# First units' queries loaded without zeros, and spread over 128 partitions by GpSimd

## The chip, the core and the metric

The kernel runs on one core of a Trainium2 chip. The time is the device time of one execution in microseconds (us). The kernel before takes 600.12 us, the median of three runs that lie between 600.06 and 600.53.

The engines are named as in the profile: PE is TensorE's matmul, PEld its weight load, DVE is VectorE, ACT is ScalarE, POOL is GpSimd, SP is SyncE, which issues the DMAs (its queue is SPq).

## The reference

Two stages follow each other: attention over chunks of a sequence with a small memory, and a feed-forward layer with a sloped ReLU.

```python
# q, k, v: (4, 8, 768, 64); mem_k, mem_v: (4, 8, 8, 64)
for c in range(768 // 32):
    q_c = q[:, :, c * 32:(c + 1) * 32]
    keys   = mem_k with k[c * 32 - 16 : c * 32 + 32 + 8]     # cut at the ends of the sequence
    values = mem_v with v[the same]
    a = softmax(q_c @ keys.T / 8)
    out[:, :, chunk c] = a @ values
x = out as (3072 tokens, 8 heads * 64)
h = x @ w_in                                   # w_in (512, 2048)
g = max(h, 0) + alpha * min(h, 0)
return g @ w_out                               # w_out (2048, 512)
```

## The kernel before

**Tiling.** The tokens are cut into 8 blocks of 384 (`BT`), and the 8 heads into 4 pairs. A *unit* is one block of one pair of heads, so there are 32 units; unit u is pair u % 4 of block u // 4. A unit has 4 times 96 queries (`TQ`), each of 3 chunks of 32. A key window of a chunk has 64 columns (`KW`: 56 of the sequence and 8 of the memory).

**The first eight units** (`NWIN`) are made in another way than the others, by `load_first`, `score_products` and `windows`, and with them this text is concerned. Their inputs lie ready in an array `first` in memory: for each unit, 128 partitions (two heads of 64) by 1824 columns of 4 bytes: 768 columns of queries (`NQ`), 544 of keys, 512 of values. The queries of a chunk take 64 columns: 32 for the one head, which are zero in the partitions of the other, and 32 for the other head. One matmul over 128 partitions then gives both heads' scores for a chunk, one under the other, with no sum between heads. There are 4 buffers (`early`, `NSET`); units 4 to 7 reuse those of units 0 to 3. These buffers lie where the last four weight blocks will go.

A unit goes through these steps. SP loads queries with keys, then values (L485). TensorE runs a few warming matmuls on a tile of ones (`stir`, L293) and 12 score matmuls (L307, each of them 2 in the profile). VectorE hides what lies outside the sequence, takes the maximum (L504) and subtracts it (`less`, L508, into one of two buffers `e`). ScalarE takes the exponential (L512). VectorE sums (L516) and inverts (L519). GpSimd scales the weights into one of two padded tiles `ew` (L529, L533). TensorE transposes them (`turn`, L541), ScalarE copies the result (L546), TensorE multiplies with the values (L554), and `split` writes the result as a high and a low part (L469 on ScalarE, L472 on VectorE), the input of the feed-forward layer.

**The feed-forward layer** takes 16 blocks of 128 hidden columns for each block of tokens. Its weights come as packed 8-byte words, one DMA of 512 KB for each of `w_in` and `w_out` for a block (L594), and ScalarE and VectorE decode them (`decode_part`: L617, L625, L629, L633, L641, L644) before TensorE uses them (L718 up, L748 down). The later 24 units of attention run in between.

**What sets the order.** The kernel adds each step to a list with its engine, an estimated cost, what it reads and writes, and how much work must follow it (`rest`). `Plan.send` plays this list through with those costs and issues the steps in the order that comes out; a DMA is taken to land 2.3 us after its issue. Each engine runs its own instructions in that order, so an instruction that waits holds up all that stand behind it on its engine. SP is such a queue, too. The costs of the first loads are

```python
step(SP, 1.6, partial(load, 0, NQ + NT * NKT), writes=[("qk", u % NSET)], rest=due(u))
step(SP, 0.78, partial(load, NQ + NT * NKT, NQ + NT * NKT + NV), writes=[("fv", u % NSET)], rest=due(u))
```

Of the kernel before, what the change touches and what calls it, by code (L numbers as in the profile page):

```python
# [9 lines left out]
F32 = mybir.dt.float32  # L10
# [8 lines left out]
P = 128  # L19
B, H, S, D = 4, 8, 768, 64  # L20
NM = 8
CH, LEFT, RIGHT = 32, 16, 8
# [3 lines left out]
NJ = TQ // CH  # L26
TK = LEFT + TQ + RIGHT
BT = 384
NHALF = B * S // BT
NT = BT // TQ  # L30
NPAIR = H // 2
# [36 lines left out]
NKT = TK + 2 * NM  # L68
STARTS = (0, LEFT + CH // 2, TK - 2 * CH + 2 * NM)

PE, DVE, ACT, POOL, SP = "PE", "DVE", "ACT", "POOL", "SP"
# [35 lines left out]

NWIN, NSET = 2 * NPAIR, 4

STARTS_WIN = (0, 2 * LEFT, NKT - KW)  # L110
NQ = NT * NJ * 2 * CH
NV = NT * 2 * D
# [64 lines left out]
def body(ctx: ExitStack, tc: tile.TileContext, qvw, kw, first, w_in, w_out, alpha, out):  # L177
    nc = tc.nc
# [12 lines left out]
    tmp = ctx.enter_context(tc.tile_pool(name="tmp", bufs=1))  # L191
# [9 lines left out]
    qk = [const.tile([P, BT + NT * NKT], F32, name=f"qk{i}") for i in range(NKB)]  # L201
# [5 lines left out]
    early = [wps[NF - NSET + i, 0].tile([P, NQ + NT * NKT + NV], F32, name="early", tag="w") for i in range(NSET)]  # L207
# [7 lines left out]
        nc.gpsimd.memset(e[:, :, KW:], 1e-9)  # L215
    for ew in ews:
        nc.gpsimd.memset(ew, 0.0)
    warm = sm.tile([P, 1], F32, name="warm")
    nc.vector.memset(warm, 0.0)
    nc.scalar.activation(out=warm, in_=warm, func=AF.Exp)  # L220
# [2 lines left out]
    step = plan.add  # L223
# [20 lines left out]
    def rest(place):  # L244
        wide = NNARROW * NF
        return (len(ORDER) - max(place, wide)) * WIDE_PAIR + max(wide - place, 0) * PAIR

    def begins(u):

        return u // NPAIR if u < NWIN else BEGIN[(u - NWIN) // 2]  # L250

    def due(u, later=0):

        return rest(begins(u) + later + (5.5 if u >= FIRST_FRONT else 0))
# [35 lines left out]
    def stir(t, num):  # L290

        for _ in range(num):
            nc.tensor.matmul(out=t, lhsT=busy[:, :P], rhs=busy, start=True, stop=True)  # L293

    def score_products(u):
        blk, pr = divmod(u, NPAIR)
        st = state[u]
        s_ps = ps_s.tile([P, 512], F32, name="s_ps", tag=f"s{u % 2}")
        stir(s_ps, STIR[0] if u == 0 else STIR[1])
        st["s"] = s_ps[:, :2 * NJ * KW].rearrange("p (n k) -> p n k", k=KW)  # L300
        t = early[u % NSET]
        q = t[:, :NQ].rearrange("p (c x) -> p c x", c=NT * NJ)
        keys = t[:, NQ:NQ + NT * NKT].rearrange("p (t k) -> p t k", t=NT)
        for n in range(2 * NJ):
            for i in range(2):
                t, j = n // NJ * 2 + i, n % NJ
                nc.tensor.matmul(  # L307
                    out=st["s"][i * 2 * CH:(i + 1) * 2 * CH, n],
                    lhsT=q[:, t * NJ + j],
                    rhs=keys[:, t, STARTS_WIN[j]:STARTS_WIN[j] + KW],  # L310
                    start=True, stop=True,
                )
# [167 lines left out]
    def load_first(u):  # L480
        blk, pr = divmod(u, NPAIR)
        t = early[u % NSET]

        def load(lo, hi):
            nc.sync.dma_start(out=t[:, lo:hi], in_=first[blk, pr, :, lo:hi])  # L485

        state[u] = {}
        step(SP, 1.6, partial(load, 0, NQ + NT * NKT), writes=[("qk", u % NSET)], rest=due(u))
        step(SP, 0.78, partial(load, NQ + NT * NKT, NQ + NT * NKT + NV), writes=[("fv", u % NSET)], rest=due(u))

    def windows(u):

        st = state[u]
        sk, tks, ak = ("s", u % 2), [("o", 0), ("o", 1)], ("o", 2) if u % 2 else "a"
# [53 lines left out]
        def values():  # L548
# [3 lines left out]
            for t in range(NT):  # L552
                for h2 in range(2):
# [4 lines left out]
                        start=True, stop=True,  # L558
                    )

        step(PE, 1.2, partial(score_products, u), reads=[("qk", u % NSET)], writes=[sk], rest=due(u))
        step(DVE, 0.66, top, writes=[sk, ("mx", u % 3)])
        step(DVE, 0.55, less, reads=[sk, ("mx", u % 3)], writes=e_keys(u))
        step(ACT, 0.52, exps, writes=e_keys(u))
# [24 lines left out]
    def load_w(f):  # L589
        def load(i):  # L590
            k, j = ((f, i), 0) if f < NAPART else ((f, 0), i)
            if k not in raw:
                raw[k] = wps[k].tile([P, 2 if f >= NAPART else 1, DM, 2], I32, name="w_t", tag="w")
            nc.sync.dma_start(out=raw[k][:, j].rearrange("p m b -> p (m b)"), in_=srcs[i][f])  # L594

        i = f - NF + NSET
        after = [("qk", i), ("fv", i)] if i >= 0 else []
        for i in range(2):
            step(SP, 1.31, partial(load, i), writes=[("r", f, i)] + after, rest=rest(place_of(f)))

    def place_of(f):
        return PLACE[0, f]
# [229 lines left out]
    def unit_begins(u):  # L832
        if u < NWIN:
            windows(u)
        else:
            if u % 2 == 0:
                scores([u, u + 1])
        if u < NWIN and u + NSET < NWIN:
            load_first(u + NSET)
        elif u >= NWIN - NKB and u + NKB < NU:  # L840
            load_unit(u + NKB)

    for u in range(NSET):
        load_first(u)
        if u == 1:
            step(SP, 0.6, partial(nc.sync.dma_start, out=al, in_=alpha), writes=["al"])
            step(DVE, 0.1, partial(nc.vector.tensor_scalar, out=rise, in0=al, scalar1=-1.0, scalar2=1.0, op0=ALU.mult,
                                    op1=ALU.add), reads=["al"], writes=["rise"])
    for f in range(NF - NSET):
        load_w(f)  # L850
# [3 lines left out]
    for f in range(NF - NSET, NF):  # L854
        load_w(f)
# [10 lines left out]
    for blk, f in ORDER:  # L866
# [25 lines left out]
        o = o_ps.setdefault((blk, f1), [])  # L892
# [12 lines left out]
def _layout(q, k, v, mem_k, mem_v, moe_w_in, moe_w_out, moe_alpha):  # L905
    import numpy as np

    nh = S // BT
    qT = q.reshape(B, NPAIR, 2, nh, BT, D).transpose(0, 3, 1, 2, 5, 4)
    pad = ((0, 0), (0, 0), (LEFT, RIGHT), (0, 0))  # L910
    kp, vp = np.pad(k, pad), np.pad(v, pad)

    def keys(x, mem, s, *spans):
        return np.concatenate([mem if p is None else x[:, :, s + LEFT + p[0]:s + LEFT + p[1]] for p in spans], axis=2)

    kwin = np.stack([keys(kp, mem_k, t * TQ, (-16, 16), None, (16, 72), None, (72, 104)) for t in range(S // TQ)],
                    axis=2)
    kwin = kwin.reshape(B, NPAIR, 2, nh, NT, NKT, D).transpose(0, 3, 1, 2, 6, 4, 5)
    vwin = np.stack([keys(vp, mem_v, t * TQ, (-16, 16), None, (16, 104)) for t in range(S // TQ)], axis=2)
    vwin = vwin.reshape(B, NPAIR, 2, nh, NT, P, D).transpose(0, 3, 1, 5, 4, 2, 6)  # L920
    nwin = NWIN // NPAIR
    qd = np.zeros((nwin, NPAIR, 2, D, NT * NJ, 2, CH), q.dtype)
    for h in range(2):
        qd[:, :, h, :, :, h] = qT.reshape(NHALF, NPAIR, 2, D, NT * NJ, CH)[:nwin, :, h]
    kfirst = np.stack([keys(kp, mem_k, t * TQ, (-16, 16), None, (16, 104), None) for t in range(S // TQ)], axis=2)
    kfirst = kfirst.reshape(B, NPAIR, 2, nh, NT, NKT, D).transpose(0, 3, 1, 2, 6, 4, 5)
    kfirst = kfirst.reshape(NHALF, NPAIR, P, NT * NKT)[:nwin]
    vparts = vwin.reshape(NHALF, NPAIR, P, NV)
    return dict(
        qvw=np.concatenate([qT.reshape(NHALF, NPAIR, P, BT), vparts], axis=3),  # L930
        kw=np.ascontiguousarray(kwin).reshape(NHALF, NPAIR, P, NT, NKT),
        first=np.concatenate([qd.reshape(nwin, NPAIR, P, NQ), kfirst, vparts[:nwin]], axis=3),
        w_in=np.ascontiguousarray(moe_w_in.reshape(NK, P, NF, P).transpose(2, 1, 0, 3)
                                  ).reshape(NF, P, NK * P).view(np.int64),
        w_out=np.ascontiguousarray(moe_w_out.reshape(NF, P, DM)).view(np.int64),
        alpha=np.ascontiguousarray(moe_alpha.reshape(NF, P).T),
    )
# [15 lines left out]
```

## Time and profile before

| | |
|---|---|
| median of three runs | 600.12 us |
| the profiled execution | 600.83 us |
| its span, first to last instruction | 599.0 us |
| PE busy | 592.1 us (99%) |
| DVE busy | 388.2 us (65%) |
| ACT busy | 211.1 us (35%) |
| POOL busy | 36.7 us (6%) |
| DMA read and written | 41.95 and 6.29 MB |

A row of the timeline or of the groups has the start or the busy time, the engine, the line, the operation, the tile written and those read (`out<-in`), and the shapes. In square brackets, or behind the last bar, stands how long the engine stood idle just before, and what ended this idle time. The busy time of TensorE is modelled at its ends, since matmuls are pipelined: a TensorE that is shown as busy may still have small gaps. Views by stage give the busy time of each engine in a stretch. The DMA rows give size and time from issue to landing.

### The profile page before, as it was taken

The page shows a single profiled execution, that of the slowest core. Times are in us where ns is not written, and L with a number is a line of the kernel's source. Part 1 is how long each engine was busy: PE and PEld are TensorE (multiplying, and loading weights), DVE is VectorE, ACT ScalarE, POOL GpSimd, SP SyncE. Part 2 cuts the span into 40 slices and gives each one's busy share as a digit, 9 for nine tenths or more (in the row PEclk, how much of TensorE's full clock was granted, in tenths as well). Part 3 has the DMA queues.
Part 4 walks back from the last instruction along what each step waited for, and adds up shares of the span by engine and source line. Part 5 has one row for each costly group of instructions (what it writes and reads, how often), then busy time and mean ns, then how long its engine had stood idle before and what let it go on. Part 6 is the DMA issues. An engine that isn't in the chain of part 4 may idle for free.

```text
span 599.0 us, 10981 instructions
## 1 busy us (share of the span) xinstructions
PE 592.1 (99%) x4430; PEld 506.3 (85%) x4430; DVE 388.2 (65%) x904; ACT 211.1 (35%) x580; POOL 36.7 (6%) x61
## 2 busy tenths in 40 slices
PE   8999999999999999999999999999999999999997
PEld 5689898988988989899898888888888888888886
DVE  5888998887958768785885852861762771530530
ACT  3688878644222414323233301302400411210201
POOL 3410000010001101010010100100100100000000
PEclk9999999999999999999999999999999999999999
DMA  8999500222040302403204003003201000000001
GB/s 325 354 402 407 236 0 1 66 65 89 2 146 8 100 5 98 143 11 100 84 17 143 11 1 92 9 0 101 69 2 36 0 1 36 36 1 0 1 1 71
DMA packets 21076, 48.96 MB, mean 82 GB/s; under 512 B 2464, under 2 KB 5792, under 8 KB 21024
## 3 DMA queue, kind: packets, MB, share of 16 engines
q1 hardware_dynamic: 20880, 48.12, 22.7%
q8 instruction: 35, 0.57, 0.4%
q10 hardware_dynamic: 144, 0.13, 0.1%
q14 instruction: 17, 0.14, 0.1%
HBM read 41.95 MB, written 6.29 MB: 81 GB/s over the span
## 4 chain that ended last, share of the span: by engine, by line
PE 96%; DMA 2%; DVE 1%; ACT 1%; issue 0%; SPq 0%; ACTq 0%
PE h_ps L718 44%; PE o_ps L748 44%; PE a_ps L433 3%; PE s_ps L332 2%; DMA w_t<-w_in 2%; PE s_ps L293 1%; PE s_ps L307 1%; PE a_ps L554 0%; DVE w_t L629 0%; ACT qk L546 0%; PE o_ps L541 0%; ACT a L617 0%; DVE w_t L625 0%; DVE xl L472 0%; SPq L485 0%
## 5 line engine op out<-in xcount | busy, mean ns | idle before, releaser
L718 PE MATMUL h_ps<-xh,w 128*128 128x384 f32 (+1 forms) x896 | 248.8, 359 | 0.3 <-DVE w L644 0.3
L718 PEld LDWEIGHTS h_ps<-xh,w 128*128 128x128 f32 x896 | 164.8, 188 | 16.6 <-DVE w L644 0.6
L748 PE MATMUL o_ps<-w,gh 128*128 128x512 f32 x528 | 162.7, 389 | 0.0
L718 PE MATMUL h_ps<-xl,w 128*128 128x384 f32 (+1 forms) x448 | 162.6, 363 | 0.1
L727 ACT ACTIVATE g<-h_ps 128x384 f32<-128x384 f32 (+1 forms) x112 | 60.7, 542 | 194.4 <-PE h_ps L718 128.6
L730 DVE SCALAR_TENSOR_TENSOR g<-g,rise,h_ps 128x384 f32<-128x384 f32 (+1 forms) x112 | 74.8, 668 | 74.5 <-ACT g L727 73.6
L748 PEld LDWEIGHTS o_ps<-w,gh 128*128 128x128 f32 x528 | 99.1, 188 | 20.4
L408 DVE STREAM_TRANSPOSE pt<-e 32x64 f32<-32x64 f32 (+1 forms) x336 | 99.4, 301 | 7.4 <-POOL e L387 2.0
L748 PE MATMUL o_ps<-w,gl 128*128 128x512 f32 x264 | 102.8, 389 | 0.0
L718 PEld LDWEIGHTS h_ps<-xl,w 128*128 128x128 f32 x448 | 84.1, 188 | 10.2 <-DVE xl L472 0.3
L748 PE MATMUL o_ps<-w,xh 128*128 128x512 f32 x240 | 74.8, 393 | 0.0
L748 PEld LDWEIGHTS o_ps<-w,gl 128*128 128x128 f32 x264 | 49.6, 188 | 10.2
L472 DVE TENSOR_TENSOR xl<-a_ps,xh 128x384 fp32r<-128x384 f32 x32 | 17.7, 557 | 59.5 <-ACT xh L469 58.8
L748 PEld LDWEIGHTS o_ps<-w,xh 128*128 128x128 f32 x240 | 45.0, 188 | 8.9
L469 ACT CAST xh<-a_ps 128x384 fp32r<-128x384 f32 x32 | 15.0, 481 | 95.7 <-PE a_ps L433 93.7
L736 DVE CAST gh<-g 128x512 fp32r<-128x512 f32 (+1 forms) x72 | 28.8, 401 | 30.6 <-PE o_ps L748 28.2
L387 POOL TENSOR_TENSOR e<-e,den 128x384 f32<-128x384 f32 x24 | 22.7, 947 | 419.8 <-DVE den L384 270.0
L740 DVE TENSOR_TENSOR gl<-g,gh 128x512 fp32r<-128x512 f32 (+1 forms) x72 | 46.6, 648 | 1.7
L366 ACT ACTIVATE e<-s_ps,mx 128x64 f32<-128x64 f32 x144 | 43.4, 318 | 11.1 <-DVE mx L358 11.1
L748 PE MATMUL o_ps<-w,xl 128*128 128x512 f32 x120 | 46.8, 390 | 0.0
L366 ACT ACTIVATION_READ_ACCUMULATOR e<-s_ps,mx 128x1 f32 x144 | 30.4, 211 | 0.0
L805 ACT COPY o_t<-o_ps 128x512 f32<-128x512 f32 x21 | 12.2, 591 | 44.6 <-PE o_ps L748 44.1
(58 smaller groups left out, 382.6 us busy)
## 6 DMA issues: line engine op xcount, KB each, us to landing
w_t<-w_in SPq DMA_DIRECT2D x16, 512.0 KB, 10.1
w_t<-w_out SPq DMA_DIRECT2D x16, 512.0 KB, 10.0
qk<-kw SPq DMA_DIRECT2D x24, 272.0 KB, 4.4
v_t<-qvw SPq DMA_DIRECT2D x24, 256.0 KB, 2.9
out<-o_t SPq DMA_DIRECT2D x23, 256.0 KB, 2.1
early<-first SPq DMA_DIRECT2D x8, 656.0 KB, 6.3
qk<-qvw SPq DMA_DIRECT2D x24, 192.0 KB, 4.9
early<-first SPq DMA_DIRECT2D x8, 256.0 KB, 6.9
```

Source lines behind the costliest of these rows:

```text
L366: nc.scalar.activation(out=st["e"][:, i], in_=st["s"][h2][:, n], func=AF.Exp, scale=SCALE, bias=d["mx"][:, u - us[0], n, h2:h2 + 1], accum ...
L387: nc.gpsimd.tensor_tensor(out=st["e"], in0=st["e"], in1=st["den"].broadcast_to([P, NJ * 2, KW]), op=ALU.mult)
L408: nc.vector.transpose(out=pts[u % NPT][quad * CH:(quad + 1) * CH, j, t0:t0 + n1 - n0].rearrange("p t h q -> p (t h) q"), in_=(st["e"], zer ...
L433: nc.tensor.matmul(out=st["a"][h2 * D:(h2 + 1) * D, t * TQ:(t + 1) * TQ], lhsT=st["v"][:, t, h2, :], rhs=pts[u % NPT][:, :, t, h2, :], sta ...
L469: nc.scalar.copy(out=ring[k][0][:, cols], in_=st["a"][:, :BT])
L472: nc.vector.tensor_tensor(out=ring[k][1][:, cols], in0=st["a"][:, :BT], in1=ring[k][0][:, cols].bitcast(F32), op=ALU.subtract)
L718: nc.tensor.matmul(out=h["ps"][:, :n_cols], lhsT=ws[f, 0][:, wk, k * P:(k + 1) * P], rhs=parts(blk, k)[1](xk), start=(k == 0 and n == 0), ...
L727: nc.scalar.activation(out=h["g"], in_=h["ps"][:, :n_cols], func=AF.Relu, scale=-1.0)
L730: nc.vector.scalar_tensor_tensor(out=h["g"], in0=h["g"], scalar=rise[:, f:f + 1], in1=h["ps"][:, :n_cols], op0=ALU.mult, op1=ALU.add)
L736: copy(out=h["gh"], in_=h["g"])
L740: nc.vector.tensor_tensor(out=h["gl"], in0=h["g"], in1=h["gh"].bitcast(F32), op=ALU.subtract)
L748: nc.tensor.matmul(out=o_ps[tt], lhsT=h[gk][:, tt * P:(tt + 1) * P], rhs=ws[f, 1][:, wk], start=(f == first_f and i == 0), stop=(f == last ...
```

## The change

The array `first` holds the queries without zeros: 384 columns of 128 partitions instead of 768. They are loaded into a tile of their own (`q_t`, in buffers that are otherwise used late for outputs). Zeros are written once into the halves of the four `early` buffers that have to be zero, by eight memsets on VectorE at the program's start (64 partitions by 384 columns each). For each unit GpSimd then copies each head's 64 partitions by 384 columns from `q_t` to its half of `early`. The keys become a DMA of their own. So a unit is loaded by three DMAs (192, 272 and 256 KB) instead of two (656 and 256 KB).

The columns of the queries are ordered anew: head, query of the chunk, chunk, where it was chunk, head, query. The 64 columns of one score matmul's stationary operand are now 12 columns apart. The score products wait for the copies as well as the keys, and the planner gets new steps with new costs. No arithmetic changes.

```diff
@@ body
     for ew in ews:
         nc.gpsimd.memset(ew, 0.0)
+    for t in early:
+        for h2 in range(2):
+            nc.vector.memset(t[(1 - h2) * D:(2 - h2) * D, h2 * BT:(h2 + 1) * BT], 0.0)
     warm = sm.tile([P, 1], F32, name="warm")
@@ score_products
-        q = t[:, :NQ].rearrange("p (c x) -> p c x", c=NT * NJ)
+        q = t[:, :NQ].rearrange("p (x c) -> p c x", c=NT * NJ)
@@ load_first
+        d = {}
+
         def load(lo, hi):
-            nc.sync.dma_start(out=t[:, lo:hi], in_=first[blk, pr, :, lo:hi])
+            nc.sync.dma_start(out=t[:, lo:hi], in_=first[blk, pr, :, lo - BT:hi - BT])
+
+        def load_q():
+            d["q"] = tmp.tile([P, BT], F32, name="q_t", tag=f"o{u % NSET}")
+            nc.sync.dma_start(out=d["q"], in_=first[blk, pr, :, :BT])
+
+        def spread(h2):
+            rows = slice(h2 * D, (h2 + 1) * D)
+            nc.gpsimd.tensor_copy(out=t[rows, h2 * BT:(h2 + 1) * BT], in_=d["q"][rows])
 
         state[u] = {}
-        step(SP, 1.6, partial(load, 0, NQ + NT * NKT), writes=[("qk", u % NSET)], rest=due(u))
-        step(SP, 0.78, partial(load, NQ + NT * NKT, NQ + NT * NKT + NV), writes=[("fv", u % NSET)], rest=due(u))
+
+        step(SP, 0.53, load_q, writes=[("tmp", u % NSET)], rest=due(u))
+        for h2 in range(2):
+            step(POOL, 0.45, partial(spread, h2), reads=[("tmp", u % NSET)], writes=[("fq", h2, u % NSET)], rest=due(u))
+        step(SP, 0.75, partial(load, NQ, NQ + NT * NKT), writes=[("qk", u % NSET)], rest=due(u))
+        step(SP, 0.7, partial(load, NQ + NT * NKT, NQ + NT * NKT + NV), writes=[("fv", u % NSET)], rest=due(u))
@@ windows
-        step(PE, 1.2, partial(score_products, u), reads=[("qk", u % NSET)], writes=[sk], rest=due(u))
+        step(PE, 1.2, partial(score_products, u), reads=[("qk", u % NSET)] + [("fq", h2, u % NSET) for h2 in range(2)], writes=[sk], rest=due(u))
@@ load_w
-        after = [("qk", i), ("fv", i)] if i >= 0 else []
+        after = [("qk", i), ("fv", i), ("fq", 0, i), ("fq", 1, i)] if i >= 0 else []
@@ _layout
-    qd = np.zeros((nwin, NPAIR, 2, D, NT * NJ, 2, CH), q.dtype)
-    for h in range(2):
-        qd[:, :, h, :, :, h] = qT.reshape(NHALF, NPAIR, 2, D, NT * NJ, CH)[:nwin, :, h]
+    qfirst = qT.reshape(NHALF, NPAIR, P, NT * NJ, CH)[:nwin].swapaxes(3, 4).reshape(nwin, NPAIR, P, BT)
```

Since the planner gets other steps, it sends instructions in another order in the first part of the program. Three places follow. The first is SP's queue up to the first weights: `early_157` to `early_160` are the buffers of units 0 to 3 and then 4 to 7, and 1312 columns are queries with keys. Before:

```order
5 L485 DMA early_157<-first 128x1312
6 L485 DMA early_158<-first 128x1312
7 L485 DMA early_157<-first 128x512
8 L485 DMA early_159<-first 128x1312
9 L485 DMA early_158<-first 128x512
10 L594 DMA w_t_327<-w_in 128x1024
```

And now, where 384 columns are queries, 544 keys and 512 values:

```order
9 L495 DMA q_t_247<-first 128x384
10 L491 DMA early_157<-first 128x544
11 L491 DMA early_157<-first 128x512
12 L495 DMA q_t_276<-first 128x384
13 L491 DMA early_158<-first 128x544
14 L491 DMA early_158<-first 128x512
15 L495 DMA q_t_307<-first 128x384
16 L491 DMA early_159<-first 128x544
17 L612 DMA w_t_326<-w_in 128x1024
```

Ahead of these stand the first loads of units 0 to 3, four DMAs before and eight now. In both orders the queries and keys of seven units and the values of two come before the first weights, in smaller pieces now.

The second place is GpSimd's queue after its first memsets, where `ew0` and `ew1` are the padded tiles of units 0 and 1. Before:

```order
11 L217 MEMSET ew0_161 128x768
12 L217 MEMSET ew1_162 128x768
13 L529 TENSOR_TENSOR ew0_161<-e_167,den_248 128x2x2x64
14 L533 TENSOR_TENSOR ew0_161<-e_167,den_248 128x2x56
15 L533 TENSOR_TENSOR ew0_161<-e_167,den_248 128x2x8
16 L529 TENSOR_TENSOR ew1_162<-e_168,den_273 128x2x2x64
```

And now, with a pair of copies for each unit (`x2`):

```order
16 L499 COPY early_160<-q_t_224 64x384 x2
17 L499 COPY early_157<-q_t_247 64x384 x2
18 L547 TENSOR_TENSOR ew0_161<-e_167,den_274 128x2x2x64
19 L551 TENSOR_TENSOR ew0_161<-e_167,den_274 128x2x56
20 L551 TENSOR_TENSOR ew0_161<-e_167,den_274 128x2x8
21 L499 COPY early_158<-q_t_276 64x384 x2
22 L547 TENSOR_TENSOR ew1_162<-e_168,den_305 128x2x2x64
23 L551 TENSOR_TENSOR ew1_162<-e_168,den_305 128x2x56
24 L551 TENSOR_TENSOR ew1_162<-e_168,den_305 128x2x8
25 L499 COPY early_159<-q_t_307 64x384 x2
```

The copies of units 0 to 4 stand ahead of the first scaling, those of unit 5 ahead of the second, and those of unit 6 ahead of the third.

The third place is VectorE's queue between the inverse for unit 1 and the maximum of unit 4; `e_167` and `e_168` are the two buffers of the exponentials (even and odd units). Before:

```order
16 L519 RECIPROCAL den_273<-den_273 128x6
17 L508 TENSOR_TENSOR e_167<-s_ps_233,mx_270 128x6x64
18 L516 TENSOR_REDUCE den_315<-e_167 128x6
19 L508 TENSOR_TENSOR e_168<-s_ps_254,mx_279 128x6x64
20 L519 RECIPROCAL den_315<-den_315 128x6
21 L502 MEMSET s_ps_295 64x8
22 L504 TENSOR_REDUCE mx_332<-s_ps_295 128x6
23 L516 TENSOR_REDUCE den_345<-e_168 128x6
24 L508 TENSOR_TENSOR e_167<-s_ps_295,mx_332 128x6x64
```

And now:

```order
20 L537 RECIPROCAL den_305<-den_305 128x6
21 L526 TENSOR_TENSOR e_167<-s_ps_258,mx_300 128x6x64
22 L526 TENSOR_TENSOR e_168<-s_ps_284,mx_312 128x6x64
23 L534 TENSOR_REDUCE den_366<-e_167 128x6
24 L520 MEMSET s_ps_332 64x8
25 L522 TENSOR_REDUCE mx_371<-s_ps_332 128x6
26 L537 RECIPROCAL den_366<-den_366 128x6
27 L534 TENSOR_REDUCE den_386<-e_168 128x6
28 L537 RECIPROCAL den_386<-den_386 128x6
29 L476 TENSOR_TENSOR xl_185<-a_ps_373,xh_184 128x384
30 L526 TENSOR_TENSOR e_167<-s_ps_332,mx_371 128x6x64
```

The subtraction for unit 3 moved ahead of the sum of unit 2, the inverse for unit 2 behind the maximum of unit 4, and the subtraction for unit 4 behind the inverse for unit 3 and unit 0's low part.

More of the change, by code (lines that the diff above doesn't have):

```diff
@@ L931, in _layout @@
         kw=np.ascontiguousarray(kwin).reshape(NHALF, NPAIR, P, NT, NKT),
-        first=np.concatenate([qd.reshape(nwin, NPAIR, P, NQ), kfirst, vparts[:nwin]], axis=3),
+        first=np.concatenate([qfirst, kfirst, vparts[:nwin]], axis=3),
         w_in=np.ascontiguousarray(moe_w_in.reshape(NK, P, NF, P).transpose(2, 1, 0, 3)
```

## The prediction

> **What bounds the kernel now.** I first asked for the busy time of each engine by stage, to see where time can be lost at all. The columns are the stretch, its length, and the busy time of PE, PEld, DVE, ACT and POOL, then the granted clock, the DMA share and GB/s.
>
> ```profile
> 0.00:36.00 36.00, 32.83 (x414) 22.87 (x416) 25.89 (x62) 20.09 (x41) 14.01 (x37) 1.00 0.93 347
> 36.00:100.00 64.00, 64.00 (x329) 58.10 (x326) 56.44 (x79) 53.42 (x69) 0.00 (x0) 1.00 0.52 208
> 100.00:200.00 100.00, 100.00 (x935) 89.72 (x934) 79.53 (x194) 41.06 (x133) 5.98 (x6) 1.00 0.20 66
> 500.00:590.00 90.00, 90.00 (x423) 74.44 (x422) 30.99 (x50) 13.38 (x24) 0.00 (x0) 1.00 0.04 16
> ```
>
> From 36 us on TensorE has no gap, and the change alters nothing that TensorE does there. So the time moves by as much as the moment at which TensorE becomes gapless, near 35 us. That TensorE is 99% busy over the whole says little; only the first 36 us count. The same view in steps of 5 us:
>
> ```profile
> 5.00:10.00 5.00, 4.72 (x79) 3.15 (x78) 3.27 (x10) 1.04 (x2) 0.27 (x1) 1.00 1.01 409
> 10.00:15.00 5.00, 4.64 (x73) 3.49 (x74) 3.90 (x12) 2.48 (x7) 2.85 (x8) 1.00 0.97 349
> 15.00:20.00 5.00, 4.79 (x83) 3.33 (x81) 3.10 (x9) 1.82 (x5) 2.49 (x8) 1.00 1.03 400
> 20.00:25.00 5.00, 4.55 (x70) 3.40 (x64) 4.42 (x10) 3.56 (x10) 1.34 (x3) 1.00 0.88 289
> 25.00:30.00 5.00, 4.69 (x52) 3.78 (x52) 4.78 (x12) 4.58 (x11) 2.60 (x5) 1.00 1.00 371
> 30.00:35.00 5.00, 4.88 (x52) 3.91 (x51) 4.93 (x9) 4.48 (x9) 2.33 (x5) 1.00 0.99 382
> ```
>
> DMA runs at its ceiling of about 409 GB/s nearly throughout. VectorE is full from 25 to 35 us (9.71 of 10), but has 1.9 us free between 15 and 20 and 0.58 between 20 and 25. Third, the chain of waits in order of time (start, length, what):
>
> ```profile
> 10.15 9.20 DMA w_t<-w_in
> 19.35 0.02 issue
> 19.37 0.02 ACT a L617
> ...
> 34.20 0.48 DVE xl L472
> 34.68 0.04 issue
> 34.72 0.79 PE h_ps L718 x3
> ```
>
> The chain runs through the first weight load, which takes 9.20 us to land behind the queries, keys and values, and ends at VectorE handing TensorE its last late tile. The timeline tells who stands still for these loads:
>
> ```profile
> 15.58 0.48 ACT L469 CAST xh<-a_ps 128x384 fp32r<-128x384 f32 x1 [0.29 <-PE a_ps L554]
> 17.89 0.56 DVE L508 TENSOR_TENSOR e<-s_ps,mx 128x384 f32<-128x384 f32 x1
> 18.11 0.88 PE L554 MATMUL a_ps<-qk,early 128*64 128x96 f32 x16 [0.21 <-DMA early<-first]
> 19.37 0.69 ACT L617 ACTIVATE a<-w_t 128x512 f32<-128x512 f32 x1 [2.89 <-DMA w_t<-w_in]
> 20.10 0.75 DVE L625 COPY w_t<-w_t 128x512 int16<-128x512 int16 x1 [1.66 <-ACT a L617]
> 21.28 0.56 DVE L516 TENSOR_REDUCE den<-e 128x6 f32<-128x390 f32 x1 [0.43 <-ACT e L512]
> 21.85 0.88 PE L554 MATMUL a_ps<-qk,early 128*64 128x96 f32 x16 [0.33 <-DVE den L516]
> ```
>
> ScalarE's wait of 2.89 us for the weights makes VectorE stand for 1.66 us, and the exponential that ScalarE does late costs VectorE 0.43 us more. TensorE loses only 0.21 and 0.33 us at the value products: its order has other work there.
>
> **What is removed: bytes.** A unit's first load shrinks from 656 KB (768 query and 544 key columns of 4 bytes on 128 partitions) to 192 + 272 KB. Over 8 units that is 1536 KB, 3.85 us at 409 GB/s. By SP's order, the loads up to and including the first weights were 7 x 656 + 2 x 256 + 512 = 5616 KB and become 7 x 464 + 2 x 256 + 512 = 4272 KB: 1344 KB or 3.4 us less, so the weights land near 16.0 instead of 19.35. In ScalarE's new order their first use follows the L469 cast that ended at 15.58 + 0.48 = 16.06, so the 2.89 us wait goes. Unit 1's values land some 4.5 us sooner by the same sum (5104 against 3296 KB ahead), so TensorE's 0.21 us goes too. The loads behind are helped, but 36 us and later has no wait to save.
>
> **What is added at the start.** Rows that price it: issue to landing of the first load (alone in its 0.9 us window) and of the least crowded 256 KB transfers, then the first instructions.
>
> ```profile
> early<-first SPq DMA_DIRECT2D x1, 656.0 KB, 4.0
> ...
> v_t<-qvw SPq DMA_DIRECT2D x24, 256.0 KB, 2.9
> out<-o_t SPq DMA_DIRECT2D x23, 256.0 KB, 2.1
> ...
> 0.74 9.36 SPq L485 DMA_DIRECT2D early<-first  x9
> 0.91 0.48 DVE L200 MEMSET busy<- 128x512 bf16 x1 [0.91 <-PEq L944]
> 1.32 1.41 POOL L217 MEMSET ew<- 128x768 f32 x2
> 1.45 3.60 PE L293 MATMUL s_ps<-busy 128*128 128x512 bf16 x8 [1.45 <-DVE warm L219]
> 4.98 1.41 PE L307 MATMUL s_ps<-early 128*64 128x64 f32 x24
> 6.58 0.56 DVE L504 TENSOR_REDUCE mx<-s_ps 128x6 f32<-128x384 f32 x1
> ```
>
> Eight memsets of 64x384 on VectorE: by columns 0.48 x 384/512 = 0.36 us at least, 0.48 at most; I take 0.4, together 3.2 us, from 1.39 to 4.6 (5.2 at most). VectorE's next work was at 6.47, so this costs nothing; without that cover it would cost 3.2 us. The first query load lands at 0.74 + 2.1 to 2.9, about 3.4 us; GpSimd is free from 1.32 + 1.41 = 2.73. Two copies follow. A copy's price is not in the trace; it lies between writing alone and two inputs:
>
> ```profile
> 30.50 0.42 POOL L578 MEMSET e<- 128x384 f32 x1
> ...
> L387 POOL TENSOR_TENSOR e<-e,den 128x384 f32<-128x384 f32 x24 | 22.7, 947 | 419.8 <-DVE den L384 270.0
> ```
>
> I take 0.5 of 0.42 to 0.95, since one input is read and nothing computed. The copies end near 4.4 (3.7 to 5.5). Keys, 464 KB in, land before the old load's 4.74. TensorE's warming matmuls last to 1.45 + 3.60 = 5.05 anyway: the first score stays at 5.0, cost 0 (at most +0.5).
>
> **What is added later.** Sixteen copies are 8 us on GpSimd (6.7 to 15.2), which worked 1.17 us a unit. Those of units 4 to 7 stand in GpSimd's queue ahead of the softmax scaling of units 0, 1, 2 and 4; behind them wait the transposes on TensorE. SP issues 8 more DMAs (9 took 9.36 us with their waits), and the query loads of units 4 to 7 wait for the copies of units 0 to 3, with keys, values and weights behind. The last of these queries lies 1584 KB in, 928 KB or 2.3 us behind the old first load's landing at 0.74 + 4.0 = 4.74, so the copies end near 7.1 + 1.0 = 8.1, and what is queued stays bound by bytes.
>
> The planner also moves VectorE's `less` (L508 before, L526 now) of unit 3 ahead of the sum of unit 2. It must wait for GpSimd's scaling of unit 1, which reads the same buffer:
>
> ```profile
> 9.73 0.62 POOL L529 TENSOR_TENSOR ew<-e,den 128x256 f32<-128x256 f32 x1 [7.00 <-DVE s_ps L500]
> ...
> 12.55 0.54 POOL L533 TENSOR_TENSOR ew<-e,den 128x112 f32<-128x112 f32 x2
> ...
> 29.02 1.23 DVE L625 COPY w_t<-w_t 128x512 int16<-128x512 int16 x1 [0.17 <-ACT a L617]
> ```
>
> With the durations above: `less` 3 at 13.15 to 13.7, sum 2 to 14.25, maximum 4 to 14.9, sum and inverse 3 to 15.8, unit 0's difference (L472 before, L476 now) after 16.06 to 16.65. Unit 2's scaling starts near 15.1 and takes 1.16, so `less` 4 runs 16.65 to 17.2, maximum 5 to 17.85, sum 4 to 18.4, `less` 5 to 18.95. Before, that ended at 17.89 + 0.56 = 18.45: a cost of 0.5. Then comes the weights' copy, at once. It stands beside a GpSimd scaling now; such a copy took 1.23 instead of 0.75 us (0.48).
>
> **Sum.** VectorE's stalls removed, 1.66 + 0.43 = 2.09; order, -0.5; the crowded copy, -0.48: **-1.1 us**. Everything behind it, up to the gapless stretch, is VectorE's full list, so the gain should survive. Its ends: at least TensorE's own waits 0.21 + 0.33 = 0.5, at most 2.1.
>
> The profiled execution took 600.83 with a span of 599.0 (1.83 outside); the three runs have a median of 600.12, so its span would be about 598.3. I subtract from the median: **599.0 us**, its own range 598.0 to 599.6.
>
> **Rivals.** The new query layout puts the 64 columns of one weight load 12 elements, 48 bytes, apart; before they were contiguous. *Slower weight loads* (rival 1, the other side):
>
> ```profile
> L307 PEld LDWEIGHTS s_ps<-early x192: 132/138/232, 5.0 to 23.8; 128*64 128x64 f32 x192
> L748 PEld LDWEIGHTS o_ps<-w,gh 128*128 128x128 f32 x528 | 99.1, 188 | 20.4
> 12.83 0.78 PEld L307 LDWEIGHTS s_ps<-early 128*64 128x64 f32 x24 [0.42 <-issue]
> ```
>
> 64 more columns cost 188 - 138 = 50 ns, 0.8 ns a column. 24 loads in 0.78 us are 32.5 ns apart, less than the 50, so two overlap. If a strided column costs double, a unit needs 24 x 50 / 2 = 0.6 us more, eight units 4.8. TensorE's gaps from 5 to 35 us could take 0.28 + 0.36 + 0.21 + 0.45 + 0.31 + 0.12 = 1.7 of it, up to 2.8 if the modelled ends hide 0.1 at each of some ten waits: +2.0 to +3.1, about 602.7. It decides from 1.35 times a column's price on, where 8 x 0.21 us exceeds the 1.7. Against it: 0.8 ns a column is slow, and nothing here tells whether packing matters at that pace. No read of TensorE in this trace is strided so, hence both ends stay, 0 and +4.8; I lean to 0.
>
> The Trainium skill (SBUF — State Buffer, Door 1: The DMA port swizzle) states 16-byte lines, of which each access that crosses to a new one pays, so that fp32 may step 4 elements for free. By that rule these loads, one line per column, pay, and the time would be rival 1's; the page names no size, and no run here shows it yet.
>
> *GpSimd late, or the loads hidden anyway* (rival 2). At 0.95 us a copy, the first score waits to 0.74 + 2.9 + 1.9 = 5.5 (+0.5), and unit 5's copies, between the scalings of units 0 and 1, end at 9.73 + 1.16 + 1.9 = 12.8, where the scaling of unit 1 ended at 13.09 and needs 1.16 more: 0.9 late. Then -1.1 + 0.5 + 0.9 = +0.3, 600.4. For it: GpSimd stands on the path of every unit; against: 3.06 us a unit still fits the 3.4 between scores.
>
> **How the numbers follow.** Forecast 0.52; rival 1 0.26 (0.03 of it far beyond, up to four times the column's price); rival 2 0.17; more gain than 2.1 (ScalarE's decoding, moved earlier, frees it too) 0.05. A measurement can tell about 0.2%, 1.2 us: below 598.9 is faster, above 601.3 slower. The forecast lies on that edge: 0.24 faster, 0.28 same. With 0.05 from the last case and 0.16 and 0.03 of the rivals within 0.2%, that is 0.29, 0.47 and 0.24. The range 598.0 to 602.9 leaves out about 0.05 below and 0.13 above.
>
> **What would show it.** Right: w_in lands before 17 us; ScalarE's first decode and VectorE's first weight copy without a DMA wait before them; the first score still at 5.0; 24 score loads in 0.78 us; the chain's last VectorE step near 33 us. Wrong: score loads spread over 1.2 us or more (rival 1); GpSimd copies of 0.8 us or scalings that wait for copies (rival 2); weights still landing after 18 us.

## The result, and the profile after

The changed kernel takes **606.89 us** (median of 4 runs, 606.86 to 606.97) against 600.27 for the kernel before on the same chip. The ratio is **1.0109, with an interval of 1.0097 to 1.0121**: it is 6.6 us slower. The forecast was 599.0, and the range ended at 602.9. The profiled execution took 606.92 with a span of 605.1. Two executions of the experiments below were far slower than all others, one of heads_w4 with 2073 us and one of the kernel before with 653 us at a lower clock, and ratios and ranges leave them out.

First the stage views of the changed kernel, columns as before:

```profile
0.00:36.00 36.00, 34.19 (x353) 25.86 (x354) 24.02 (x64) 17.12 (x34) 20.49 (x52) 1.00 0.84 278
50.00:60.00 10.00, 9.42 (x47) 7.89 (x45) 8.75 (x14) 8.80 (x13) 0.00 (x0) 1.00 1.03 408
```

TensorE now has only 1.81 us of gaps in the first 36 us (3.17 before), and a new gap of 0.58 us between 50 and 60 us, where the kernel before had none. A TensorE that is busier and yet ends later does some work more slowly. The weight loads of the score line say which (durations in ns, shortest, median and longest, then the starts):

```profile
L311 PEld LDWEIGHTS s_ps<-early x192: 207/237/240, 5.0 to 29.4; 128*64 128x64 f32 x192
```

One weight load takes 237 ns instead of 138, and the last starts at 29.4 instead of 23.8. The timeline, for one unit's 24 loads and for the steps that the prediction spoke of:

```profile
4.98 1.71 PEld L311 LDWEIGHTS s_ps<-early 128*64 128x64 f32 x24 [0.84 <-POOL early L499]
9.62 1.70 PEld L311 LDWEIGHTS s_ps<-early 128*64 128x64 f32 x24 [0.42 <-issue]
...
1.54 3.90 DVE L221 MEMSET early<- 64x384 f32 x8
3.23 1.06 POOL L499 COPY early<-q_t 64x384 f32<-64x384 f32 x2 [0.50 <-DMA q_t<-first]
11.43 0.62 POOL L547 TENSOR_TENSOR ew<-e,den 128x256 f32<-128x256 f32 x1
19.68 0.73 ACT L635 ACTIVATE a<-w_t 128x512 f32<-128x512 f32 x1
```

The 24 loads of a unit take 1.71 us where they took 0.78: 0.93 more. Only the first unit had taken longer before, 1.27:

```profile
4.98 1.27 PEld L307 LDWEIGHTS s_ps<-early 128*64 128x64 f32 x24 [0.84 <-DMA early<-first]
```

So eight units cost 7 x 0.93 + 0.44 = 7.0 us more. ScalarE's first decode (L635) no longer waits for a DMA, but it is not earlier than before (19.68 against 19.37), since everything behind the scores is late. The weights themselves land at 18.3 instead of the forecast 16.0: their load is issued at 11.87 (10.15 before), behind loads that wait for the late scores to free their buffers. The chain of waits has lost its DMA; a piece of it past the first stage (start, length, what) is new:

```profile
57.11 0.51 ACT xh L754
57.62 0.96 ACT w L659
58.58 0.39 ACT g L745
58.97 0.02 issue
58.99 0.61 DVE g L748
59.60 0.48 DVE xl L758
```

There ScalarE casts decoded weights (L659) ahead of the ReLU part `g` (L745) that VectorE and TensorE need. So two things had to be told apart from what the prediction counted: the weight loads, and the order that the planner makes of the new steps.

### The profile page after: what moved, and what is told of

It is laid out like the page before. It is cut to its first block, busy times and chain, and to the rows that moved or that the text cites. A ratio compares the mean times of both kernels' runs of the same rounds, so it can differ in the third digit from the quotient of the medians.

```text
span 605.1 us, 11029 instructions
## 1 busy us (share of the span) xinstructions
PE 598.9 (99%) x4430; PEld 512.8 (85%) x4430; DVE 391.0 (65%) x912; ACT 211.3 (35%) x580; POOL 43.6 (7%) x77
## 4 chain that ended last, share of the span: by engine, by line
PE 98%; DVE 0%; ACT 0%; issue 0%; ACTq 0%
PE h_ps L736 44%; PE o_ps L766 43%; PE a_ps L437 3%; PE s_ps L311 2%; PE s_ps L336 2%; PE s_ps L297 1%; PE a_ps L572 1%; PE o_ps L559 1%; PE o_ps L297 0%; ACT w L659 0%; DVE g L748 0%; ACT o_t L823 0%; DVE mx L522 0%; ACT xh L754 0%; DVE busy L201 0%
## 5 line engine op out<-in xcount | busy, mean ns | idle before, releaser
L745 ACT ACTIVATE g<-h_ps 128x384 f32<-128x384 f32 (+1 forms) x112 | 60.5, 540 | 194.3 <-PE h_ps L736 128.9
L748 DVE SCALAR_TENSOR_TENSOR g<-g,rise,h_ps 128x384 f32<-128x384 f32 (+1 forms) x112 | 74.9, 669 | 74.0 <-ACT g L745 73.2
```

The lines of the kernel that those rows point to most:

```text
L745: nc.scalar.activation(out=h["g"], in_=h["ps"][:, :n_cols], func=AF.Relu, scale=-1.0)
L748: nc.vector.scalar_tensor_tensor(out=h["g"], in0=h["g"], scalar=rise[:, f:f + 1], in1=h["ps"][:, :n_cols], op0=ALU.mult, op1=ALU.add)
```

## The experiments

All of these kernels do the whole computation. The kernel before, run beside them, has medians of 600.24 to 600.40.

### Only the column order undone (packed)

The change stays, but the 64 columns of a chunk lie side by side again; memsets and copies write 12 runs of 32 columns instead. The order on the engines is that of the change. Here and below, `...` stands for lines left out.

```diff
-        q = t[:, :NQ].rearrange("p (x c) -> p c x", c=NT * NJ)
+        q = t[:, :NQ].rearrange("p (c x) -> p c x", c=NT * NJ)
-            nc.gpsimd.tensor_copy(out=t[rows, h2 * BT:(h2 + 1) * BT], in_=d["q"][rows])
+            nc.gpsimd.tensor_copy(out=t[rows, :NQ].rearrange("p (c h x) -> p c h x", h=2, x=CH)[:, :, h2],
+                                  in_=d["q"][rows].rearrange("p (c x) -> p c x", x=CH))
...
```

> The changed kernel with one thing undone: the 64 columns of a score matmul's weights lie side by side again, so the memsets and GpSimd's copies write 12 runs of 32 columns. Loads, zeros, copies and the order of all engines are those of the changed kernel. Theory 1 (the whole loss is TensorE's weight loads at a step of 48 bytes): 24 score loads take 0.78 us again instead of 1.71, and the time falls from 606.9 to the forecast's 599.0, between 598.0 and 599.6. Rival (the loss comes from the planner's new order, GpSimd's copies or the smaller DMAs): the loads take 0.78 us but the time stays above 604.

Measured: **601.13 us** (11 runs), ratio 1.0014 [1.0006, 1.0023]. Of this kernel:

```profile
L311 PEld LDWEIGHTS s_ps<-early x192: 132/138/227, 5.0 to 23.5; 128*64 128x64 f32 x192
...
11.00 0.62 POOL L548 TENSOR_TENSOR ew<-e,den 128x256 f32<-128x256 f32 x1
17.29 0.69 ACT L636 ACTIVATE a<-w_t 128x512 f32<-128x512 f32 x1 [0.68 <-DMA w_t<-w_in]
37.45 0.39 PE L767 MATMUL o_ps<-w,xl 128*128 128x512 f32 x1
...
50.00:60.00 10.00, 9.26 (x45) 7.51 (x44) 9.03 (x13) 8.15 (x12) 0.00 (x0) 1.00 1.03 408
```

And of the kernel before:

```profile
38.44 0.39 PE L748 MATMUL o_ps<-w,xl 128*128 128x512 f32 x1
...
50.00:60.00 10.00, 10.00 (x54) 9.26 (x53) 9.03 (x13) 8.22 (x12) 0.00 (x0) 1.00 1.03 407
```

The weight loads are back at 138 ns, and 606.89 - 601.13 = 5.8 us with them. The time lies between the two expectations: the strided columns explain most of the loss, but the forecast gain is not there either. It was there for a while: the first weights land at 17.27 instead of 19.35, and the first down product that TensorE does (L767) starts at 37.45, while L748 started at 38.44 in the kernel before. Then TensorE gets through only 45 matmuls between 50 and 60 us, 54 before: the same ScalarE order as in the changed kernel, seen in its chain:

```profile
51.23 0.51 ACT xh L755
51.74 0.96 ACT w L660
52.70 0.40 ACT g L746
53.10 0.02 issue
53.12 0.61 DVE g L749
53.74 0.48 DVE xl L759
```

### Only the column order changed (step2, step3, step4, step6, step12)

The kernel before, with its zeros and its loads, and the 64 columns of a chunk 2, 3, 4, 6 or 12 elements (8 to 48 bytes) apart.

```diff
+STEP = 12
-        q = t[:, :NQ].rearrange("p (c x) -> p c x", c=NT * NJ)
+        q = t[:, :NQ].rearrange("p (g x s) -> p g s x", x=2 * CH, s=STEP)
-                    lhsT=q[:, t * NJ + j],
+                    lhsT=q[:, (t * NJ + j) // STEP, (t * NJ + j) % STEP],
...
```

> The kernel before with the column order alone changed: queries are loaded with their zeros, but the 64 columns of a score matmul's weights lie 12 elements (48 bytes) apart. Theory 1: 24 score loads take 1.7 us, eight units cost 8 x 0.93 = 7.4 us, less what TensorE's gaps take up (1.7 to 2.8): 604.8 to 606.2. Rival: the strided loads are hidden where no copies and no new order come with them: 600.3 within 1.2.

> The kernel before with the columns 4 elements (16 bytes) apart, so each on a 16-byte line of its own, next to those of three other chunks. If the step in bytes decides and 4 fp32 are free, as the Trainium skill (SBUF — State Buffer, Door 1: The DMA port swizzle) says: 24 loads in 0.78 us and 600.3. If one column per line is what pays: 24 loads in 1.7 us and the time of the kernel with a step of 12.

> The kernel before with the columns 2 elements (8 bytes) apart, two columns to a 16-byte line. If a load pays by the line: 24 loads in 0.78 us and 600.3 us. If it pays by bytes spanned: a fraction more, about 0.85 us, and 600.5 to 601. If anything but side by side pays in full: 1.7 us and the time of the kernel with a step of 12.

> The kernel before with the 64 columns of a chunk's weights 3 elements (12 bytes) apart, all else as before. Steps of 8, 16 and 48 bytes gave 138, 217 and 237 ns for one weight load. Theory A (the price is paid once the columns are farther apart than 8 bytes, whatever the distance): 210 ns or more, about 604 us. Theory B (the price rises with the distance between 8 and 16 bytes): 165 to 195 ns, 601 to 602.5 us.

> The kernel before with the 64 columns of a chunk's weights 6 elements (24 bytes) apart, all else as before. Theory A (price flat beyond 16 bytes, with a small rise): 217 to 237 ns for one weight load, 604 to 605.7 us. Theory B (the number of lines touched counts, so that 24 bytes lies between 16 and 48 in proportion): near 222 ns. Theory C (multiples of 16 bytes are the bad case): under 200 ns and under 603 us.

| columns apart | runs | median, us | ratio to before |
|---|---|---|---|
| 4 bytes (before) | | 600.3 | |
| 8 bytes (step2) | 10 | 600.30 | 1.0001 [0.9992, 1.0010] |
| 12 bytes (step3) | 8 | 601.83 | 1.0022 [1.0012, 1.0032] |
| 16 bytes (step4) | 4 | 604.20 | 1.0065 [1.0050, 1.0081] |
| 24 bytes (step6) | 2 | 603.60 | 1.0054 [1.0036, 1.0072] |
| 48 bytes (step12) | 4 | 605.65 | 1.0091 [1.0077, 1.0105] |

The same row of each kernel, from step2, step3, step4, step6 and step12 in this order:

```profile
L308 PEld LDWEIGHTS s_ps<-early x192: 135/138/225, 5.0 to 23.2; 128*64 128x64 f32 x192
```

```profile
L308 PEld LDWEIGHTS s_ps<-early x192: 164/177/223, 5.0 to 25.6; 128*64 128x64 f32 x192
```

```profile
L308 PEld LDWEIGHTS s_ps<-early x192: 193/217/218, 5.0 to 28.4; 128*64 128x64 f32 x192
```

```profile
L308 PEld LDWEIGHTS s_ps<-early x192: 187/208/217, 4.9 to 27.3; 128*64 128x64 f32 x192
```

```profile
L308 PEld LDWEIGHTS s_ps<-early x192: 207/237/243, 5.0 to 29.5; 128*64 128x64 f32 x192
```

The column order alone costs 5.3 us at the change's 48 bytes. The price of a load starts between 8 and 12 bytes and rises with the distance, but not evenly: 24 bytes is a little cheaper than 16 (208 against 217 ns; in the times alone their intervals overlap). What sets it beyond 16 bytes, these five points don't tell. step12, step2 and theory B of step3 came out as expected; step4 lies between its two cases, and step6's 208 ns is outside all three of its theories.

### The packed kernel in before's order (packed_order)

As packed, but the planner is told of one load of queries and keys at the old cost, and of the copies as steps of cost 0 with no delay behind them. TensorE, ScalarE and VectorE then run before's steps in before's order (VectorE with the eight memsets added), and GpSimd does the copies of units 4 to 7 ahead of the scalings of units 1, 2, 3 and 5.

```diff
-        step(SP, 0.53, load_q, writes=[("tmp", u % NSET)], rest=due(u))
+        step(SP, 1.6, load_both, writes=[("qk", u % NSET)], rest=due(u))
-            step(POOL, 0.45, partial(spread, h2), reads=[("tmp", u % NSET)], ...)
+            step(POOL, 0.0, partial(spread, h2), reads=[("qk", u % NSET)], ...)
-        step(SP, 0.75, partial(load, NQ, NQ + NT * NKT), ...)
...
```

> The changed kernel with the columns of a chunk side by side (so the weight loads should stay near 0.78 us per 24) and with the copies told to the planner as steps of cost 0, so that TensorE, ScalarE and VectorE run the steps of before in before's order; on GpSimd the copies stand ahead of the first scalings as before. Theory A (the forecast's gain of some 1 us is there at 37 us, and the planner's other order on ScalarE, the weights' cast ahead of the ReLU part at 51 to 54 us, gives it back): no TensorE gap over 0.2 us between 50 and 60 us, and 599.0 to 599.7 us. Theory B (the gain is lost in the first 36 us, to copies ahead of the scalings on GpSimd and to the queries landing later): TensorE busy under 33.2 of the first 36 us and 600.3 us or more, with or without a gap at 50 us.

Measured: **600.00 us** (11 runs), ratio 0.9993 [0.9984, 1.0002]. Half of each theory holds. Theory A's gap is gone:

```profile
0.00:36.00 36.00, 32.26 (x416) 23.24 (x421) 27.96 (x71) 20.62 (x43) 21.78 (x53) 1.00 0.87 303
5.00:10.00 5.00, 4.01 (x81) 2.57 (x78) 3.81 (x13) 1.25 (x3) 3.32 (x7) 1.00 1.02 352
50.00:60.00 10.00, 10.00 (x52) 9.17 (x52) 9.22 (x13) 8.00 (x11) 0.00 (x0) 1.00 1.03 408
```

52 matmuls instead of 45, at 10.00 / 52 = 0.19 us each, are 1.3 us, and the time fell by 1.13 against packed. So the order was worth that. But 600.00 is 0.3 us under before where theory A has 0.6 to 1.3, and TensorE is busy for only 32.26 of the first 36 us, as theory B has it. Its own reasons, copies ahead of the scalings and late queries, do not show: the first scaling starts at 9.59, before at 9.73, and no unit's scores start later than before. The timeline of this kernel and the chain in order of time show another:

```profile
16.67 0.69 ACT L639 ACTIVATE a<-w_t 128x512 f32<-128x512 f32 x1 [0.34 <-DMA w_t<-w_in]
18.20 0.92 DVE L647 COPY w_t<-w_t 128x512 int16<-128x512 int16 x1
28.71 0.67 ACT L639 ACTIVATE a<-w_t 128x512 f32<-128x512 f32 x1 [1.56 <-DMA w_t<-w_in]
29.41 0.77 DVE L647 COPY w_t<-w_t 128x512 int16<-128x512 int16 x1 [2.29 <-ACT a L639]
```

```profile
20.91 0.83 PE a_ps L576 x16
21.75 0.02 issue
21.76 0.33 SPq L491
22.09 0.04 issue
22.13 6.50 DMA w_t<-w_in
```

The first weights come nearly when they should (decoded from 16.67 instead of 19.37), and VectorE's first weight copy stands at 18.20 instead of 20.10: 1.9 us ahead of the profiled execution of before. But the third weight load is issued at 22.13, behind a value load (L491) that stands in SP's queue until TensorE has done a unit's value products and its buffer is free. The view of SP's waits adds these up (total, times, longest, in us):

```profile
SPq L491 <- PE a_ps L576: 6.6, 4, 2.7
```

VectorE gets there early and waits 2.29 us. At its next steps it is 1.0 us ahead, no more.

How much of this lead is the change's? The profiled execution of before took 600.83, 0.7 us above the median. step2 has the same loads and the same order, its weight loads take 138 ns, and its profiled execution took 600.09, near the median. It is a second look at the start before:

```profile
18.53 0.67 ACT L618 ACTIVATE a<-w_t 128x512 f32<-128x512 f32 x1 [1.92 <-DMA w_t<-w_in]
19.23 0.76 DVE L626 COPY w_t<-w_t 128x512 int16<-128x512 int16 x1 [0.67 <-ACT a L618]
20.40 0.56 DVE L517 TENSOR_REDUCE den<-e 128x6 f32<-128x390 f32 x1 [0.40 <-ACT e L513]
28.76 0.91 DVE L626 COPY w_t<-w_t 128x512 int16<-128x512 int16 x1 [0.79 <-ACT a L618]
37.59 0.39 PE L749 MATMUL o_ps<-w,xl 128*128 128x512 f32 x1
```

Against it packed_order is 1.0 us ahead at the first weight copy and 0.14 at TensorE's first down product (37.45 against 37.59). In step2, too, VectorE already waits 0.79 us for the third weight load.

### Those weight loads issued earlier (packed_order_w4, before_w4)

The second and third weight load are issued ahead of unit 4's value load, which is the first that waits for TensorE's value products. Nothing else moves. The control does the same to the kernel before.

```diff
+        early = [self.weights[0, 1], self.weights[1, 0]]
+        order = [n for n in order if n not in early]
+        i = order.index(self.values[4])
+        for n in order[:i] + early + order[i:]:
+            self.steps[n][2]()
...
```

> The kernel with packed columns in before's order (packed_order, 600.0 us), with one thing moved: on the load queue, the second and third weight load (w_out of slice 0 and w_in of slice 1) are issued ahead of the value load of unit 4, which waits for TensorE to free its buffer. In packed_order the first weights land at 16.65 us instead of 19.35, but these two are issued at 20.4 and 22.1 us, and VectorE then waits 2.29 us for the third. Theory A (the bytes saved become time only if the loads behind them are issued earlier too; an in-order queue that waits for TensorE's buffers holds them): the 2.29 us wait is gone or under 0.5 us, and 598.3 to 599.3 us. Theory B (the wait moves elsewhere, TensorE or VectorE being full by then): 599.7 to 600.3 us. Theory C (the value loads now come late): over 600.3 us.

> The control: the kernel before with its full 656 KB unit loads and only the two weight loads moved ahead of the value load of unit 4. Its transfers run at 409 GB/s without a gap to 20 us, so the queue's order can bring no bytes sooner. Theory A (bytes bound the start there, and the third weight load only comes to be waited for once they are saved): 600.0 to 600.8 us, no difference; 0.5 to 2 us slower if the value loads come late. Theory B (the queue's order alone is worth the gain, with or without the smaller loads): 598.5 to 599.5 us.

Measured: **599.43 us** for packed_order_w4 (11 runs, 599.03 to 599.80), ratio 0.9985 [0.9976, 0.9995]; 600.03 for before_w4, ratio 0.9996 [0.9987, 1.0005]. Of packed_order_w4:

```profile
17.70 0.68 ACT L648 ACTIVATE a<-w_t 128x512 f32<-128x512 f32 x1 [0.96 <-DMA w_t<-w_in]
27.40 0.69 ACT L648 ACTIVATE a<-w_t 128x512 f32<-128x512 f32 x1
28.12 0.76 DVE L656 COPY w_t<-w_t 128x512 int16<-128x512 int16 x1 [0.60 <-ACT a L648]
37.08 0.39 PE L779 MATMUL o_ps<-w,xl 128*128 128x512 f32 x1
```

The wait of 2.29 us shrank to 0.60, and TensorE's first down product starts at 37.08 instead of 37.45, although the first weights are decoded at 17.70 instead of 16.67. This version beats both kernels: 0.9 us under before, about what had been forecast for the change, though just short of the 0.2% that the prediction asked for. Theory A's time is 0.1 off its upper end and the wait 0.1 over its 0.5, but its mechanism is there. With the full loads the same move brings nothing that can be told from no change. The two were run side by side, and their runs don't overlap (599.03 to 599.80 against 599.89 to 600.84): with the weight loads moved, the smaller loads are worth 0.6 us. What the move alone brings is less sure: packed_order ran on another chip, and the intervals of the two ratios overlap.

### No zeros and no copies (heads, heads_w4)

The queries are loaded once, without zeros, with the keys in one load of 464 KB; each score product is done as two, one for each head's 64 partitions.

```diff
+                for h2 in range(2):
+                    rows, at_ = slice(h2 * D, (h2 + 1) * D), (2 * i + h2) * CH
                     nc.tensor.matmul(
-                        out=st["s"][i * 2 * CH:(i + 1) * 2 * CH, n],
-                        lhsT=q[:, t * NJ + j],
+                        out=st["s"][at_:at_ + CH, n],
+                        lhsT=q[rows, t * NJ + j],
...
```

> The kernel before with no zeros at all: queries and keys of a unit in one load of 464 KB instead of 928, no copies and no memsets, and the 12 score products of a unit done as 24, each over the 64 partitions of one head, with 32 weight columns instead of 64; all other work in before's order. Theory A (a score product over 64 partitions costs about what the later head products of the same kind show, some 0.6 us per unit for 24 of them, against 0.78 for the 12 full ones, and the bytes saved let the first weights land near 16 us): 598.0 to 599.2 us. Theory B (24 products cost twice 12, 1.6 us per unit, as the strided columns did): +0.8 us a unit, some of it in TensorE's gaps, 603 to 606 us. Theory C (loads are hidden anyway, nothing else changes): 600.0 to 600.6.

> The kernel without zeros whose score products go head by head (heads, 599.79 us; 48 products of 64 partitions per unit instead of 24 of 128), with the same two weight loads moved ahead of the value load of unit 4. In heads VectorE waits 1.68 us for the third weight load, at 28.2 us. Theory A (the held load is what eats the gain): that wait is gone or under 0.5 us, and 598.2 to 599.2 us. Theory B (another wait takes its place): 599.5 to 600.1 us. Theory C (value loads late): over 600.3 us.

Measured: 599.79 us for heads, ratio 0.9992 [0.9984, 1.0001], and 600.07 for heads_w4 (10 runs), ratio 0.9992 [0.9983, 1.0001]: neither can be told from the kernel before. Theory A's price for the products of heads holds, its time does not. A unit's products, and a row of the value products of unit 1, in the timeline of heads_w4; last, the same row in heads:

```profile
20.53 0.87 PE L315 MATMUL s_ps<-early 64*32 64x64 f32 x48
19.51 0.55 PE L563 MATMUL a_ps<-qk,early 128*64 128x96 f32 x8 [0.74 <-issue]
...
19.22 0.55 PE L555 MATMUL a_ps<-qk,early 128*64 128x96 f32 x8 [0.45 <-issue]
```

48 of them take 0.87 us, where 24 full ones take 0.92 in packed_order. In heads VectorE waits 1.68 us at the same weight load as in packed_order. With the loads moved (heads_w4) that wait is 0.67, but TensorE stops for 0.74 us in the middle of a unit's value products, where it stopped for 0.45 before the move. The time is theory B's; its mechanism, another wait in place of the one removed, is seen only in part. What TensorE stops for is open: the row names only "issue", and the values of this unit had landed by 16.5 (issued at 10.59, 5.9 us), so they did not come late.

### The strided kernel in before's order (after_order)

The edit of packed_order, made to the changed kernel, whose columns stay 48 bytes apart.

> The changed kernel, its weight columns 48 bytes apart as in the change, with only the order of the steps put back to before's (the copies told to the planner as steps of cost 0, as in packed_order). Theory A (the two costs add up: 1.1 us for the planner's order, as between packed at 601.13 and packed_order at 600.00, and the rest for the strided weight loads): the ScalarE stall at 57 us is gone and 605.5 to 606.0 us, about step12's 605.65. Theory B (with the strided loads TensorE is full from 5 us on, and the order matters only where it is not): 606.6 to 607.1 us.

Measured: **605.80 us** (4 runs, 605.75 to 606.03), ratio 1.0093 [1.0076, 1.0110]. Theory A: TensorE has no gap from 36 to 100 us, and the order is worth 606.89 - 605.80 = 1.1 us here as well. step12, with before's loads and zeros, took 605.65: with strided columns the bytes saved bring nothing.

## Why the prediction was wrong

The four kernels with and without strided columns, in the new and the old order, make the balance, in medians:

| | strided columns | columns side by side | difference |
|---|---|---|---|
| the planner's new order | 606.89 | 601.13 | 5.8 |
| before's order | 605.80 | 600.00 | 5.8 |
| difference | 1.1 | 1.1 | |

From 600.27 that is +5.8 for the weight loads, +1.1 for the order, and -0.3 for what the bytes brought: 606.9.

**The strided weight load** is the step that failed: "both ends stay, 0 and +4.8; I lean to 0". The reason given, that 0.8 ns a column is slow, was no reason; the load is slow, and strided it is slower still. The mechanism was rival 1's, and its terms can be checked one by one. The column's price: taken as double, 0.6 us a unit. Measured were 99 ns more a load, on the 50 ns that 64 columns had been put at: three times the price, not double, and 0.93 us a unit, so that 24 x 0.099 / 0.93 = 2.6 loads overlap where two were taken. TensorE's gaps: taken to absorb 1.7 to 2.8; 7.0 - 5.8 = 1.2 and 7.0 - 5.3 = 1.7 were absorbed, so the 0.1 us that each modelled end was to hide does not show. With the measured 7.0 and the lower absorption rival 1 would have read 7.0 - 1.7 = +5.3. Of the 0.26 given to it only 0.03 lay that far out, so the upper end of the range was too low as well: it rested on a doubling that no row supported.

The Trainium skill (SBUF — State Buffer, Door 1: The DMA port swizzle) had spoken against the change by its 16-byte lines. Its direction was right at 48 bytes. The same place asks for at least two accesses to each line, which gives 8 bytes for fp32, and the runs agree: 138 ns at 8 bytes, 177 at 12. Its own reading of this as four free fp32 elements does not fit: at 16 bytes the load took 217 ns. At 12 bytes every second column is alone on its line (those at 0 and 12 share one, those at 24 and 36 do not), and the 39 ns there are half of the 79 at 16 bytes, where each is alone. At 24 and 48 bytes each is alone as well, and the load costs 70 and 99 ns more, so the lines are not the whole of it.

**The gain itself, 2.09 us of stalls, was too large** by half. It was read from one execution, 0.7 us above the median, and then taken from the median. In that execution the DMAs moved only 349 GB/s between 10 and 15 us; in step2's they moved 380, and VectorE's two stalls are 0.67 + 0.40 = 1.07 us there (0.64 + 0.41 in before_w4). With these the forecast's own sum, less its 0.5 for the order and 0.48 for the crowded copy, is 0.1 us of gain.

**"So the gain should survive"** failed too, in two places. The order: the prediction followed the moved steps on VectorE up to the weight copy, and priced them at 0.5 us, but looked at no order behind that. The planner, given steps of other costs, also sent ScalarE's weight cast ahead of `g` at 51 to 57 us, inside the stretch that I had called gapless and left alone. That was 1.1 us. The next load: VectorE's full list was taken to follow at once, though its second weight copy (L625 at 29.02) stood right behind a ScalarE step that needs the third weight load. I said that SP's queue "stays bound by bytes". From 18 to 22 us it was bound by buffers that TensorE frees. Against step2, a lead of 1.0 us at the first weight copy became 0.14 behind this load. packed_order_w4, with the load issued earlier, lies 0.6 under the same move in the kernel before.

**What held.** The first weights: foretold at 16.0, they were decoded from 16.67 in packed_order and 17.29 in packed. They are that late because the bytes did not move at the 409 GB/s of the sum: from 5 to 10 us packed_order's DMAs are as full as before (1.02) and move 352. Whether the smaller pieces cause this, no run tells. ScalarE's wait of 2.89 us was gone in the changed kernel and 0.34 in packed_order; VectorE's 1.66 and 0.43 were gone with it in packed_order. The first score stayed at 5.0 (4.98). The eight memsets were hidden, though a single one took 3.90 / 8 = 0.49 us, a little over my bound. A GpSimd copy took 1.06 / 2 = 0.53, taken at 0.5. Rival 2's price, late scalings, did show in the changed order: 11.00 for the first scaling in packed, against 9.73; in before's order it did not (9.59). The changed kernel's 11.43 is mostly the strided loads, since step12, without any copies, has 11.18.

**What stays open.** How the 1.1 us of the order divide among the engines was not tested apart: packed and packed_order also differ on GpSimd and SP. That they are lost at ScalarE's cast rests on the place: from 36 to 50 us packed gets through 75 matmuls and packed_order through 73, from 50 to 60 us through 45 and 52, and the gap there is gone in before's order. And a gain of 0.3 us is near what one execution differs from the next by: packed_order's interval includes no change.

## What to carry to other kernels

Before an operand of TensorE is laid out anew, price its weight load from the distance of its columns: here 8 bytes were free, 12 cost 39 ns on 138, and 48 cost 99, which TensorE, nearly full, could not hide. Before a stall is counted as gain, look at it in a second execution: here it was half as long in one near the median. Bytes that are saved become time only up to the next load that stands in an in-order queue behind something that isn't bytes; look for that load, and what it waits for, before counting the gain. Where a planner sets the order, new steps and costs move instructions far behind the place of the edit, so every engine's order has to be compared to its end, not only where the change is.

## What was not expected of the hardware

A weight load of 64 fp32 columns over 128 partitions took 138 ns at 4 and 8 bytes from column to column, 177 at 12, 217 at 16, 208 at 24 and 237 at 48: neither a step at 16 bytes nor a steady rise. And 48 score products over 64 partitions and 32 columns took no longer (0.87 us) than 24 over 128 partitions and 64 columns (0.92).
